# A planner that keeps GpSimd off VectorE's wide operations, and float64 conversion spread over fourteen chunks

## The chip, the cores and the metric

One core of one Trainium2 chip runs the whole program in one launch. The metric is the device time of that launch in microseconds (us), as the median of three runs. A difference of about 0.2% is the least that a measurement of this kernel can tell from no change.

## The reference

Three parts follow each other on 2304 tokens of width 512.

```
scores = q @ k.T / 8 - slope[h] * distance      # 8 heads, 576 positions, window 128, causal
attn   = softmax(scores) @ v                    # becomes x, 2304 x 512
P      = 8 rounds of row and column scaling of exp(x @ w_gate)
out    = sum over 8 experts of P[:, e] * (relu(x @ w1[e]) @ w2[e])       # 512 -> 1024 -> 512
result = leaky(out @ w_in, 0.01) @ w_out        # 512 -> 2048 -> 512
```

`w_in` and `w_out` come as float64 and are made into float32 on the chip, in 32 pieces of 128 x 512.

## The kernel before

**Work.** The two dense layers are 20 chunks of 512 hidden columns: 16 for the experts (two for each), 4 for the last layer. A chunk runs over five token groups (`PAIRS`: four of 512 tokens, one of 256), first through its half of the first matrix (`a_steps`, matmuls at L1089), then of the second (`b_steps`, L1205). Each product of 2 x 2 blocks is formed with 7 block products instead of 8 (`PRODUCTS`), and each of those is three fp16 matmuls, of high and low parts of both factors. A steady chunk is some 800 matmuls. TensorE (PE) runs nearly without a break; the other engines evict and combine its results and prepare the next chunk's weights.

**Who does what around TensorE.** ScalarE (ACT) copies the first block products out of PSUM (L1101 `q<-s`), VectorE (DVE) adds later ones (L1105 `sq<-s,q`) and writes the low parts of h (L1117). ACT and GpSimd (POOL) make high and low parts: L1158 and L1161 for h, L803 and L804 for weights. In `b_steps`, DVE adds results to the accumulators (L1218), or ACT and POOL share that (L1215, then L1216). POOL also makes the sums of weight blocks (L964).

**Float64 pieces** (`to_single`). A piece is loaded, and then runs through DVE L1018 (exponent bits), ACT L1021, DVE L1024 (sign), DVE L1029 (mantissa bits), ACT L1030, ACT L1036, POOL L1038 and L1042, and a store to DRAM. L1018, L1024 and L1029 read and write SBUF alone. `side_jobs(ci + 1, n)` puts n pieces beside the weights of the chunk after `ci`; before the change n is 3 for chunks 1 to 10 and 2 for chunk 11, and then the 32 pieces are done. The first piece of a chunk uses buffer `raw0` (in the rows `raw_173`), the others `raw1` (`raw_174`).

**The order.** The kernel is written as a stream of steps, and at its end a planner (`Plan`) sets the order of the instructions of each engine. `depend` finds who needs whom. `deadlines` gives each node the latest time by which it should end, counted back from matmuls that run without a break. `order` is a list scheduler: at each step it takes the engine that can go on first, and for it the ready node with the earliest deadline; `fix` writes the order into the program. Each engine then works through its own list in that order, and a late instruction holds up all that stands behind it on its engine.

`weigh` marks DVE nodes that work from SBUF to SBUF as `shared`: a price that `takes` raises when such a node would start while POOL is at work, and POOL's price rises when it would start while such a DVE node is at work. Both are prices in the planner's sums alone; nothing in the program makes POOL wait for DVE or DVE for POOL, other than data:

```python
            elif node["shared"] and gpsimd[0] <= t < gpsimd[1]:
                cost = max(cost, gpsimd[1] - t + cost - node["shared"])
            elif node["eng"] == "Pool" and port[0] <= t < port[1]:
                cost += max(0.0, port[1] - t - 140)
```

Of the kernel before, what the change touches and what calls it, by code (L numbers as in the profile page):

```python
# [30 lines left out]
class Plan:  # L31
# [13 lines left out]
    LANDING = 2000.0  # L45
    PER_NS = 350.0
    NEAR = 60.0

    def __init__(self, nc, tc, slots, before, after):
        self.tc = tc  # L50
# [192 lines left out]
    def deadlines(self, products):  # L243


        nodes = self.nodes
        n = len(nodes)
        ends, t, mode = {}, 0.0, "full"
        for i in products:
            t += nodes[i]["cost"] + self.TURN.get((mode, nodes[i]["mode"]), 0)  # L250
            mode = nodes[i]["mode"]
            ends[i] = t
        latest = [ends.get(i, t + 5000) for i in range(n)]
        left = [len(self.behind[i]) + len(self.softly[i]) for i in range(n)]
        room = dict.fromkeys(self.START, t + 5000)
        heap = [(-latest[i], -i) for i in range(n) if not left[i]]
        heapq.heapify(heap)
        while heap:
            i = -heapq.heappop(heap)[1]
            a = nodes[i]  # L260
            eng = a["eng"]
            if eng not in ("PE", "SP"):
                latest[i] = min(latest[i], room[eng])
                room[eng] = latest[i] - a["cost"] + self.START[eng]
            for k in a["before"] | a["starts"] | a["soft"]:
                b = nodes[k]
                end = latest[i] - a["cost"] + (b["cost"] if k in a["starts"] else -self.latency(b, a))
                latest[k] = min(latest[k], end)
                left[k] -= (k in a["before"]) or (k in a["starts"])
                left[k] -= k in a["soft"]  # L270
                if not left[k]:
                    heapq.heappush(heap, (-latest[k], -k))
        return latest

    def order(self, latest):
        nodes, behind = self.nodes, self.behind
        n = len(nodes)
        left = [len(node["before"]) + len(node["starts"]) for node in nodes]
        ready, free = [0.0] * n, dict.fromkeys(self.START, 0.0)
# [5 lines left out]
        empty = {tag: [0.0] * bufs for tag, bufs in self.room.items()}  # L285
        using = {name: len(u) for name, u in self.users.items()}
        closed = dict.fromkeys(self.users, 0.0)
        gpsimd, port, mode = (0.0, 0.0), (0.0, 0.0), "full"
        self.starts = [0.0] * n

        def since(i):

# [9 lines left out]
        def takes(i, t):  # L302

            node = nodes[i]
            cost = node["cost"]
            if node["eng"] == "PE":
                cost += self.TURN.get((mode, node["mode"]), 0)
            elif node["shared"] and gpsimd[0] <= t < gpsimd[1]:
                cost = max(cost, gpsimd[1] - t + cost - node["shared"])
            elif node["eng"] == "Pool" and port[0] <= t < port[1]:  # L310
                cost += max(0.0, port[1] - t - 140)
            return cost

        for _ in range(n):
            choices = []
            for e, w in waiting.items():
                when = [(x, i) for x, i in ((since(i), i) for i in w) if x is not None]
                if when:
                    choices.append((max(free[e], min(when)[0]), e, when))
            t, eng, when = min(choices)  # L320
            at = dict((i, x) for x, i in when)
            near = t + (self.NEAR if eng != "PE" else 0)
            pick = min((i for i in at if at[i] <= near), key=lambda i: (latest[i], i))
# [2 lines left out]
            if eng != "PE" and eng != "SP":  # L326

                for i in sorted((i for i in at if i != pick and at[i] < start + cost), key=lambda i: latest[i]):
                    s = max(at[i], t)
                    c = takes(i, s)  # L330
                    if (latest[i] < latest[pick] and max(at[i], start + cost) + nodes[i]["cost"] > latest[i]
                            and s + c + nodes[pick]["cost"] <= latest[pick]):
                        pick, start, cost = i, s, c
                        break
                if nodes[pick]["shared"] and cost > nodes[pick]["cost"] + 100:
                    other = [i for i in at if i != pick and not nodes[i]["shared"] and at[i] <= start + 100
                             and max(t, at[i]) + nodes[i]["cost"] + cost <= max(latest[pick], start + cost + 200)]
                    if other:
                        pick = min(other, key=lambda i: latest[i])
                        start = max(t, at[pick])  # L340
# [2 lines left out]
            end = start + cost  # L343
            if eng == "PE":
                mode = node["mode"]
            elif node["shared"]:
                port = (max(start, gpsimd[1]) if gpsimd[0] <= start < gpsimd[1] else start), end
            elif eng == "Pool":
                gpsimd = start, end
            self.starts[pick] = start  # L350
            free[eng] = end - (self.START[eng] if cost > 100 else 0)
            waiting[eng].remove(pick)
# [13 lines left out]
        self.length = end  # L366
        return orders

    def fix(self):
        follows = mybir.DependencyInfo(mybir.DependencyClass.NoSync, mybir.DependencyReason.DATA)  # L370
        products = [i for i, node in enumerate(self.nodes) if node["eng"] == "PE"]
        for picks in self.order(self.deadlines(products)).values():
            line = [ins for i in picks for ins in self.nodes[i]["ins"]]
            for a, b in zip(line, line[1:]):
                self.tc.add_manual_dep(b, a.name, follows, reason="order")


@with_exitstack
def attn_moe_kernel(
# [1022 lines left out]
    for n, u in enumerate(units + [None]):  # L1402
# [20 lines left out]
        if u is not None and ci >= 1:  # L1423
            if n and units[n - 1][0] != ci and ci != NCE:
                weigh(ci)
            if p == 4:
                side += side_jobs(ci + 1, 3 if ci < NCE - 1 else 0) if ci + 1 < NC else []
        if prev[0] == NCE:
            weigh_pair(*prev)
        seq = merge(a, b) if a else b  # L1430
# [63 lines left out]
```

## Time and profile before

| | |
|---|---|
| median of three runs | 1856.25 us (1854.02 to 1857.41) |
| the profiled execution | 1853.38 us, of which its span 1851.6 us |
| busy share of the span | PE 98%, DVE 74%, ACT 73%, POOL 71% |
| mean granted TensorE clock | 0.996 of full speed |

The profiled execution is 2.9 us shorter than the median and 0.6 us shorter than the fastest of the three runs. In the rows below, PE is the matmul engine, "idle before" in square brackets is the time for which the engine did nothing before that row, with what ended it, and PEclk is the share of TensorE's full clock that was granted (1.00 is 2.4 GHz, 0.50 is 1.2 GHz). The first 250 us hold attention, mixed with chunk 0; chunks 1 to 15 follow at some 84 us each; the last layer begins at about 1430 us.

### The profile page before, as it was taken

Reading aid. Unit: us, or ns where it says so; the run is one execution under the profiler, and the core shown is the slowest. Engines: PE = TensorE matmul, PEld = TensorE weight load, DVE = VectorE, ACT = ScalarE, POOL = GpSimd, SP = SyncE. Lnnn points to the kernel's source line nnn. Section 1 sums busy time; section 2 is a strip of 40 time slices with the busy share of each in tenths; the row PEclk is TensorE's granted clock in tenths of the full one; section 3 lists DMA queues with packets and bytes.
Section 4 is the critical chain, followed back from the end, with each engine's and each line's share of the span. In section 5 each row is a group of like instructions: output and inputs, shape, how many; then the busy total and the mean of one; then the engine's idle time right before and its main releaser. Section 6 shows DMA issues by size and latency. Waiting matters only on the chain.

```text
span 1851.6 us, 45040 instructions
## 1 busy us (share of the span) xinstructions
PE 1812.1 (98%) x17542; PEld 1603.7 (87%) x17542; DVE 1367.5 (74%) x3656; ACT 1348.8 (73%) x3099; POOL 1323.0 (71%) x1154
## 2 busy tenths in 40 slices
PE   8899999999999999999999999999999999999999
PEld 6677888889888888889888888889898888989888
DVE  7878677777777687777777776666676888687877
ACT  8988778767767766767767667666666789877664
POOL 3943878787869788787868777676667696776753
PEclk9999999999999999999999999999999999999999
DMA  8332020311112121202111110100000000101002
GB/s 296 109 115 76 4 81 28 87 37 62 53 47 67 32 74 37 86 27 72 53 47 53 47 52 30 47 24 24 24 24 34 15 24 24 47 1 47 1 33 72
DMA packets 61096, 97.81 MB, mean 53 GB/s; under 512 B 4561, under 2 KB 27601, under 8 KB 60881
## 3 DMA queue, kind: packets, MB, share of 16 engines
q1 hardware_dynamic: 60880, 94.93, 15.6%
q8 instruction: 137, 2.24, 0.5%
q14 instruction: 79, 0.64, 0.1%
HBM read 81.81 MB, written 13.11 MB: 51 GB/s over the span
## 4 chain that ended last, share of the span: by engine, by line
PE 76%; POOL 7%; ACT 6%; DVE 5%; DMA 4%; issue 2%; SPq 0%; POOLq 0%; DVEq 0%; ACTq 0%
PE t L1205 36%; PE s L1089 20%; PE sq L1089 15%; POOL w L804 3%; DMA raw<-in_moe_w_dram 3%; POOL h L1161 1%; PE s L570 1%; PE o L669 1%; PE pt L651 1%; ACT junk L937 1%; POOL xp L804 1%; DVE s L1117 1%; DVE raw L1018 1%; ACT raw L940 1%; DVE acc L1218 1%
## 5 line engine op out<-in xcount | busy, mean ns | idle before, releaser
L1205 PE MATMUL t<-w,h 128*128 128x256 f16 x7560 | 953.3, 273 | 7.5 <-ACT acc L1212 2.7
L1089 PEld LDWEIGHTS <-w 128*128 128x128 f16 x8400 | 757.0, 98 | 101.5 <-issue 22.9
L1205 PEld LDWEIGHTS <-h 128*128 128x128 f16 x7560 | 736.1, 98 | 97.1 <-issue 8.8
L1089 PE MATMUL s<-xp,w 128*128 128x256 f16 (+1 forms) x4872 | 591.3, 262 | 13.4 <-ACT q L1101 10.2
L1218 DVE SCALAR_TENSOR_TENSOR acc<-t,pu,acc 128x256 f32<-128x256 f32 x866 | 407.3, 479 | 173.5 <-PE t L1205 149.9
L1161 POOL TENSOR_TENSOR h<-s,h 128x1024 f16<-128x1024 f32 x180 | 386.2, 2145 | 135.1 <-ACT h L1158 95.4
L1089 PE MATMUL sq<-xp,w 128*128 128x256 f16 (+1 forms) x3528 | 429.9, 262 | 1.8 <-ACT q L1101 1.0
L1216 POOL TENSOR_TENSOR acc<-acc,part 128x256 f32<-128x256 f32 x322 | 238.9, 743 | 201.0 <-ACT part L1215 131.5
L804 POOL TENSOR_TENSOR w<-raw,w 128x512 f16<-128x512 f32 x240 | 274.7, 1162 | 28.8 <-ACT w L803 28.3
L1101 ACT ACTIVATE q<-s 128x256 f32<-128x256 f32 x364 | 138.6, 381 | 134.9 <-PE s L1089 132.3
L1158 ACT ACTIVATE h<-s 128x1024 f16<-128x1024 f32 x180 | 190.1, 1056 | 45.8 <-DVE s L1117 44.4
L1117 DVE SCALAR_TENSOR_TENSOR h<-sq,h 128x512 f16<-128x512 f32 x352 | 193.1, 553 | 34.0 <-ACT h L1136 24.4
L1215 ACT ACTIVATE part<-t,pu 128x256 f32<-128x256 f32 x322 | 152.1, 472 | 79.8 <-PE t L1205 75.0
L1105 DVE SCALAR_TENSOR_TENSOR sq<-s,q 128x256 f32<-128x256 f32 x176 | 75.8, 431 | 143.5 <-PE s L1089 86.3
L1105 DVE SCALAR_TENSOR_TENSOR sq<-sq,q 128x256 f32<-128x256 f32 x352 | 150.3, 427 | 38.1 <-PE sq L1089 33.6
L803 ACT ACTIVATE w<-raw 128x512 f16<-128x512 f32 x240 | 147.5, 631 | 12.1 <-PE s L1089 4.3
L1117 DVE SCALAR_TENSOR_TENSOR s<-sq,s 128x256 f32<-128x256 f32 x352 | 146.4, 416 | 0.7
L1136 ACT ACTIVATE h<-sq 128x512 f16<-128x512 f32 x176 | 104.9, 596 | 55.6 <-DVE sq L1105 46.5
L1117 DVE SCALAR_TENSOR_TENSOR s<-sq,q 128x256 f32<-128x256 f32 x352 | 137.1, 417 | 9.4 <-ACT q L1113 7.8
L940 ACT ACTIVATE raw<-raw,sr 128x512 f32<-128x512 f32 x160 | 109.7, 720 | 7.4 <-DVE sr L795 7.4
L937 ACT ACTIVATE junk<-raw 128x512 bf16<-128x512 f32 x160 | 100.4, 627 | 14.6 <-DMA raw<-in_moe_w_dram 9.1
L964 POOL TENSOR_TENSOR raw<-raw 128x512 f32<-128x512 f32 x80 | 102.4, 1280 | 0.0
(151 smaller groups left out, 1682.9 us busy)
## 6 DMA issues: line engine op xcount, KB each, us to landing
raw<-in_moe_w_dram SPq DMA_DIRECT2D x32, 768.0 KB, 4.7
k_t<-in_k_dram SPq DMA_DIRECT2D x16, 512.0 KB, 4.6
raw<-in_moe_w_dram SPq DMA_DIRECT2D x32, 256.0 KB, 3.6
raw<-in_moe_w_in_dram SPq DMA_DIRECT2D x16, 512.0 KB, 3.5
raw<-in_moe_w_out_dram SPq DMA_DIRECT2D x16, 512.0 KB, 3.5
q_t<-in_q_dram SPq DMA_DIRECT2D x18, 256.0 KB, 2.9
acc<-in_v_dram SPq DMA_DIRECT2D x18, 256.0 KB, 6.1
v_t<-in_v_dram SPq DMA_DIRECT2D x18, 256.0 KB, 2.7
```

What stands on the lines that cost most here:

```text
L803: nc.scalar.activation(out=hi, in_=src, func=AF.Copy)
L804: return nc.gpsimd.tensor_tensor(out=lo, in0=src, in1=hi, op=ALU.subtract)
L1089: nc.tensor.matmul(d[b][:, f, :], t[:, wp, kk, ft * P:(ft + 1) * P], XP[p][:, o, kk, xp, :], start=(i == 0 and f == 0 and j in FIRST), sto ...
L1101: nc.scalar.activation(out=q[:, k], in_=ps, func=AF.Copy, scale=CS)
L1105: nc.vector.scalar_tensor_tensor(out=block(k), in0=ps, scalar=CS, in1=q[:, k], op0=ALU.mult, op1=ALU.add)
L1117: nc.vector.scalar_tensor_tensor(out=out, in0=in0, scalar=sc, in1=in1, op0=op0, op1=op)
L1158: nc.scalar.activation(out=h[:, 3:7, 0, :], in_=d["s"], func=AF.Copy)
L1161: nc.gpsimd.tensor_tensor(out=h[:, 3:7, 1, :], in0=d["s"], in1=h[:, 3:7, 0, :], op=ALU.subtract)
L1205: nc.tensor.matmul(ps, h[:, o, hp, f, tt * P:(tt + 1) * P], w[:, wp, ft, :], start=(i == 0 and j in FIRST), stop=(i == 5), skip_group_chec ...
L1215: nc.scalar.activation(out=part, in_=ps, func=AF.Copy, scale=s)
L1216: nc.gpsimd.tensor_tensor(out=dst, in0=dst, in1=part, op=ALU.add)
L1218: nc.vector.scalar_tensor_tensor(out=dst, in0=ps, scalar=s, in1=dst, op0=ALU.mult, op1=ALU.add)
```

## The change

Three things in the planner and one number.

1. POOL's extra price is gone. In its place `order` remembers the last shared DVE node that no POOL node has followed yet (`holder`). The next POOL node starts, in the plan, 78 ns after that node's end. If its start lies less than 1500 ns after that node got the port, the pair goes into `turns`, and `fix` makes each pair a wait in the program (`DependencyClass.Sync`): POOL's instruction waits on a semaphore of DVE's.
2. When POOL is about to be given a node, `claim` looks whether a shared DVE node of more than 230 ns could start within 400 ns; if no urgent node of DVE or POOL would be late for it, DVE's node goes first. A shared DVE node that would start while POOL works, and has time, is put off until POOL is done.
3. `lag` is by how much TensorE is behind the plan without breaks; deadlines are compared with it added.
4. Pieces: 3 in each of chunks 1 to 4, 2 in each of chunks 5 to 14, again 32.

```diff
+    REACH = 400.0
+    GUARD = 1500.0
...
-            elif node["eng"] == "Pool" and port[0] <= t < port[1]:
-                cost += max(0.0, port[1] - t - 140)
...
+                if e == "DVE" and gpsimd[1] > free[e]:
+                    when = [(max(x, gpsimd[1]) if nodes[i]["shared"] and gpsimd[0] <= max(x, free[e]) < gpsimd[1]
+                             and latest[i] + lag > gpsimd[1] + nodes[i]["cost"] else x, i) for x, i in when]
...
+            if eng == "Pool":
+                if holder is not None:
+                    t = max(t, port[1] + self.TO["Pool"])
+                first = min((i for _, i in when if since(i) <= t + self.NEAR), key=lambda i: (latest[i], i), default=None)
+                wanted = self.claim(choices, latest, lag, free["DVE"], t, first)
+                if wanted is not None:
+                    eng, when = "DVE", [wanted]
+                    t = max(free["DVE"], wanted[0])
...
+                lag = max(lag, end - self.ends[pick])
             elif node["shared"]:
                 port = (max(start, gpsimd[1]) if gpsimd[0] <= start < gpsimd[1] else start), end
+                holder = pick
             elif eng == "Pool":
                 gpsimd = start, end
+                if holder is not None and start < port[0] + self.GUARD:
+                    self.turns.append((pick, holder))
+                holder = None
...
+    def claim(self, choices, latest, lag, free, t, first):
+        for _, e, when in choices:
+            if e == "DVE":
+                for x, i in sorted(when, key=lambda w: latest[w[1]]):
+                    a = self.nodes[i]
+                    start = max(free, x)
+                    if a["shared"] and a["cost"] > 230 and start <= t + self.REACH:
...
+                        return x, i
+        return None
...
+        after = mybir.DependencyInfo(mybir.DependencyClass.Sync, mybir.DependencyReason.DATA)
+        for i, k in self.turns:
+            self.tc.add_manual_dep(self.nodes[i]["ins"][0], self.nodes[k]["ins"][-1].name, after, reason="port")
...
-                side += side_jobs(ci + 1, 3 if ci < NCE - 1 else 0) if ci + 1 < NC else []
+                side += side_jobs(ci + 1, (3 if ci < 5 else 2) if ci < NCE - 1 else 0) if ci + 1 < NC else []
```

The changed file has 39 lines more above `to_single`: L1018 is L1057 there, L1024 L1063, L1029 L1068, L1161 L1200, L1216 L1255, L1218 L1257, L964 L1003, L804 L843.

**First place: the first piece of chunk 9.** POOL in the kernel before, around the weight sums that run there (`t` is a buffer for sums, `acc` an accumulator tile):

```order
L964 TENSOR_TENSOR t_12486<-raw_174 128x512 [waits Pool_49]
L1161 TENSOR_TENSOR h<-s,h 128x4x256 [waits Activation_49]
L964 TENSOR_TENSOR raw_174<-raw_174,t_12486 128x2x256 [waits Pool_49]
L1216 TENSOR_TENSOR acc_110<-acc_110,part 128x256 [waits DVE_49,Activation_49]
L964 TENSOR_TENSOR raw_174<-raw_174 128x2x256
L1216 TENSOR_TENSOR acc_112<-acc_112,part 128x256 [waits Activation_49]
L1038 TENSOR_TENSOR raw_173<-raw_173 128x512 [waits DMAHW7_49,Activation_49]
```

DVE in the kernel before, around that piece's three operations:

```order
L1218 SCALAR_TENSOR_TENSOR acc_109<-t_13893,pu,acc_109 128x256 [waits PE_49,Pool_49]
L1218 SCALAR_TENSOR_TENSOR acc_110<-t_13996,pu,acc_110 128x256 [waits PE_49]
L1018 TENSOR_SCALAR raw_173<-raw_173 128x512 [waits DMAHW1_49,Pool_49]
L1105 SCALAR_TENSOR_TENSOR sq<-sq,q 128x256 [waits PE_49,Activation_49]
L1218 SCALAR_TENSOR_TENSOR acc_109<-t_13893,pu,acc_109 128x256 [waits PE_49]
L1024 SCALAR_TENSOR_TENSOR raw_173<-raw_173,sign 128x512 [waits Activation_49]
L1029 TENSOR_SCALAR raw_173<-raw_173 128x512 [waits DMAHW2_49]
L1105 SCALAR_TENSOR_TENSOR sq<-s_13988,q 128x256 [waits DVE_49,PE_49,Activation_49]
```

POOL in the changed kernel, around the same piece (`w` is a weight tile):

```order
L1255 TENSOR_TENSOR acc_109<-acc_109,part 128x256 [waits Activation_49]
L1200 TENSOR_TENSOR h<-s,h 128x4x256 [waits DVE_49]
L843 TENSOR_TENSOR w_13868<-raw_173,w_13868 128x512 [waits Activation_49]
L1255 TENSOR_TENSOR acc_107<-acc_107,part 128x256 [waits DVE_49]
L1200 TENSOR_TENSOR h<-s,h 128x4x256 [waits DVE_49,Activation_49]
L1003 TENSOR_TENSOR raw_174<-raw_174,t_13725 128x2x256 [waits Pool_49]
L1255 TENSOR_TENSOR acc_110<-acc_110,part 128x256 [waits Activation_49]
L1003 TENSOR_TENSOR raw_174<-raw_174 128x2x256
L1077 TENSOR_TENSOR raw_173<-raw_173 128x512 [waits DMAHW1_49,Pool_49]
```

DVE in the changed kernel, there:

```order
L1156 SCALAR_TENSOR_TENSOR s<-sq,s 128x256 [waits DVE_49]
L1257 SCALAR_TENSOR_TENSOR acc_109<-t_13853,pu,acc_109 128x256 [waits PE_49,Pool_49]
L1057 TENSOR_SCALAR raw_173<-raw_173 128x512 [waits DMAHW3_49,DMAHW1_49,Pool_49]
L1156 SCALAR_TENSOR_TENSOR s<-sq,s 128x256 [waits DVE_49]
L1257 SCALAR_TENSOR_TENSOR acc_107<-t_13909,pu,acc_107 128x256
L1257 SCALAR_TENSOR_TENSOR acc_110<-t_13956,pu,acc_110 128x256 [waits PE_49]
L1063 SCALAR_TENSOR_TENSOR raw_173<-raw_173,sign 128x512 [waits Activation_49]
L1068 TENSOR_SCALAR raw_173<-raw_173 128x512 [waits DMAHW4_49]
L1144 SCALAR_TENSOR_TENSOR sq<-sq,q 128x256 [waits PE_49]
L1257 SCALAR_TENSOR_TENSOR acc_109<-t_13853,pu,acc_109 128x256
```

Before, POOL's `t`, `h`, `raw` stand behind each other with waits for ACT and POOL alone while L1018 is due on DVE. Now POOL's `acc_107` and the `h` behind it wait for DVE, and the sums that followed stand behind those two. In chunks 5 to 14 this pattern stands ten times.

**Second place: the first low parts of h, in attention.** POOL in the kernel before:

```order
L804 TENSOR_TENSOR w_735<-raw_174,w_735 128x512 [waits Activation_49]
L618 TENSOR_TENSOR pieces<-pieces 128x8 [waits DVE_49,PE_49]
L618 TENSOR_TENSOR pieces<-pieces 128x8 [waits Pool_49]
L1161 TENSOR_TENSOR h<-s,h 128x4x256 [waits Activation_49]
L804 TENSOR_TENSOR w_738<-raw_174,w_738 128x512 [waits Activation_49]
L804 TENSOR_TENSOR w_741<-raw_174,w_741 128x512 [waits Activation_49]
L1161 TENSOR_TENSOR h<-s,h 128x4x256 [waits Activation_49]
L538 MEMSET dist 64x192 [waits Activation_49,Pool_49]
```

POOL in the changed kernel:

```order
L657 TENSOR_TENSOR pieces<-pieces 128x8 [waits DVE_49,PE_49]
L657 TENSOR_TENSOR pieces<-pieces 128x8 [waits DVE_49,Pool_49]
L843 TENSOR_TENSOR w_729<-t_681,w_729 128x512 [waits DVE_49,Activation_49]
L1200 TENSOR_TENSOR h<-s,h 128x4x256 [waits DVE_49,Activation_49] x2
L843 TENSOR_TENSOR w_732<-raw_174,w_732 128x512 [waits Activation_49]
L843 TENSOR_TENSOR w_735<-raw_174,w_735 128x512 [waits Activation_49]
L843 TENSOR_TENSOR w_738<-raw_174,w_738 128x512 [waits Activation_49]
L843 TENSOR_TENSOR w_741<-raw_174,w_741 128x512 [waits Activation_49]
```

The two `h` now stand next to each other, ahead of the last four weight parts instead of among them, and `pieces`, `w` and `h` wait for DVE.

In the whole program 217 rows of POOL name a wait for DVE before, and 255 now; where POOL waited for DVE anyway, a row shows nothing new.

## Rows read from the trace of the kernel before

**Rows 1.** The page's busy times over the whole span.

```profile
PE 1812.1 (98%) x17542; PEld 1603.7 (87%) x17542; DVE 1367.5 (74%) x3656; ACT 1348.8 (73%) x3099; POOL 1323.0 (71%) x1154
```

**Rows 2.** Windows of 100 us: PE, PEld, DVE, ACT, POOL busy, PEclk, DMA share, GB/s.

```profile
600.00:700.00 100.00, 99.65 (x954) 89.47 (x953) 74.46 (x189) 72.01 (x156) 76.83 (x65) 1.00 0.20 64
...
900.00:1000.00 100.00, 94.75 (x888) 83.87 (x887) 75.32 (x174) 65.16 (x142) 75.25 (x64) 0.98 0.15 51
1000.00:1100.00 100.00, 97.42 (x955) 87.88 (x954) 74.04 (x180) 71.18 (x156) 78.11 (x66) 1.00 0.19 64
1100.00:1200.00 100.00, 99.78 (x975) 89.61 (x973) 67.31 (x179) 68.05 (x150) 66.55 (x58) 1.00 0.11 36
1200.00:1300.00 100.00, 99.79 (x957) 89.72 (x956) 68.90 (x184) 67.23 (x147) 70.67 (x60) 1.00 0.07 22
```

**Rows 3.** PE's waits: 900 to 1000 us, 1000 to 1100 us, the whole span.

```profile
PE s L1089 <- ACT q L1101: 4.4, 2, 2.2
...
PE s L1089 <- ACT q L1101: 2.6, 1, 2.6
...
PE t L1205 <- POOL h L1161: 1.6, 1, 1.6
```

**Rows 4.** Timeline from 902 us: start, us, engine, line, operation; POOL, DVE, ACT, PE.

```profile
902.13 1.29 POOL L964 TENSOR_TENSOR t<-raw 128x512 f32<-128x512 f32 x1
903.36 2.14 POOL L1161 TENSOR_TENSOR h<-s,h 128x1024 f16<-128x1024 f32 x1
905.45 1.28 POOL L964 TENSOR_TENSOR raw<-raw,t 128x512 f32<-128x512 f32 x1
...
903.05 3.96 DVE L1018 TENSOR_SCALAR raw<-raw 128x512 int32<-128x512 int32 x1
...
907.04 0.72 ACT L1021 ACTIVATE raw<-raw,shift 128x512 int32<-128x512 int32 x1 [4.03 <-DVE raw L1018]
907.67 0.36 ACT L1101 ACTIVATE q<-s 128x256 f32<-128x256 f32 x1
...
908.09 0.38 PE L1089 MATMUL s<-xp,w 128*128 128x256 f16 x2 [2.21 <-ACT q L1101]
```

**Rows 5.** Timelines of DVE and PE, one and two chunks later.

```profile
989.63 3.97 DVE L1018 TENSOR_SCALAR raw<-raw 128x512 int32<-128x512 int32 x1
...
994.68 0.49 PE L1089 MATMUL s<-xp,w 128*128 128x256 f16 x3 [2.21 <-ACT q L1101]
...
1076.50 4.33 DVE L1018 TENSOR_SCALAR raw<-raw 128x512 int32<-128x512 int32 x1
...
1081.91 0.49 PE L1089 MATMUL s<-xp,w 128*128 128x256 f16 x3 [2.58 <-ACT q L1101]
```

**Rows 6.** Short windows, columns as in rows 2.

```profile
80.00:90.00 10.00, 7.00 (x79) 4.90 (x73) 9.06 (x14) 7.96 (x23) 7.94 (x7) 0.71 0.42 133
...
184.00:190.00 6.00, 4.18 (x23) 2.91 (x23) 3.27 (x8) 4.94 (x11) 6.00 (x5) 0.72 0.00 0
990.00:1000.00 10.00, 7.79 (x57) 6.20 (x55) 7.77 (x11) 4.47 (x10) 6.26 (x6) 0.83 0.01 2
```

**Rows 7.** Timelines of POOL and DVE, one chunk before rows 4.

```profile
819.05 1.26 POOL L964 TENSOR_TENSOR t<-raw 128x512 f32<-128x512 f32 x1
820.28 2.31 POOL L1161 TENSOR_TENSOR h<-s,h 128x1024 f16<-128x1024 f32 x1
...
819.95 0.65 DVE L1018 TENSOR_SCALAR raw<-raw 128x512 int32<-128x512 int32 x1
```

**Rows 8.** All of L1018 (ns min/median/max), and one case of DVE's timeline.

```profile
L1018 DVE TENSOR_SCALAR raw<-raw x32: 414/650/4328, 234.1 to 1100.7; 128x512 int32<-128x512 int32 x32
...
672.55 2.29 DVE L1018 TENSOR_SCALAR raw<-raw 128x512 int32<-128x512 int32 x1
```

**Rows 9.** Timelines of DVE and PE in attention.

```profile
82.96 4.53 DVE L1117 SCALAR_TENSOR_TENSOR h<-q,h 128x768 f16<-128x768 f32 x2
...
83.09 0.66 PE L651 MATMUL pt<-ident,e 128*128 128x128 f32 x4 [1.15 <-DVE pb L656]
...
86.73 2.96 PE L1205 MATMUL t<-w,h 128*128 128x256 f16 x13 [1.56 <-POOL h L1161]
```

More of the change, by code (lines that the diff above doesn't have):

```diff
@@ L252, in deadlines @@
             ends[i] = t
+        self.ends = ends
         latest = [ends.get(i, t + 5000) for i in range(n)]
@@ L287, in order @@
         closed = dict.fromkeys(self.users, 0.0)
-        gpsimd, port, mode = (0.0, 0.0), (0.0, 0.0), "full"
+        gpsimd, port, mode, holder = (0.0, 0.0), (0.0, 0.0), "full", None
         self.starts = [0.0] * n
+        self.turns = []
+        lag = 0.0
         def since(i):
@@ L330, in order @@
                     c = takes(i, s)
-                    if (latest[i] < latest[pick] and max(at[i], start + cost) + nodes[i]["cost"] > latest[i]
-                            and s + c + nodes[pick]["cost"] <= latest[pick]):
+                    if (latest[i] < latest[pick] and max(at[i], start + cost) + nodes[i]["cost"] > latest[i] + lag
+                            and s + c + nodes[pick]["cost"] <= latest[pick] + lag):
                         pick, start, cost = i, s, c
@@ L336, in order @@
                     other = [i for i in at if i != pick and not nodes[i]["shared"] and at[i] <= start + 100
-                             and max(t, at[i]) + nodes[i]["cost"] + cost <= max(latest[pick], start + cost + 200)]
+                             and max(t, at[i]) + nodes[i]["cost"] + cost <= max(latest[pick] + lag, start + cost + 200)]
                     if other:
@@ L367, in order @@
         return orders
+    def claim(self, choices, latest, lag, free, t, first):
[5 more added lines that the diff above has]
+                    if a["shared"] and a["cost"] > 230 and start <= t + self.REACH:
+                        late = start + a["cost"]
+                        if any(k != i and max(y, late) + self.nodes[k]["cost"] > latest[k] + lag and latest[k] < latest[i]
+                               and y <= late for y, k in when):
+                            return None
+                        if first is not None and latest[first] < latest[i] and late + self.nodes[first]["cost"] > latest[first] + lag:
+                            return None
+                        return x, i
+        return None
     def fix(self):
```

## The prediction

> **What bounds the kernel now.** I read the page's busy times first. PE is busy for 1812.1 of 1851.6 us, and no other engine passes 74% [rows 1]. So at most 39.5 us of idle PE, and whatever TensorE lost at half clock, can be won back; shorter work on another engine is worth nothing by itself. The windows of 100 us show where those microseconds lie. Around 650 and 1250 us PE is busy for 99.65 and 99.79 of 100 us, with and without float64 pieces beside it; from 900 to 1100 us it falls to 94.75 and 97.42 [rows 2]. That is the one place in the steady part with something to win.
>
> PE's waits say what is missing there: `s` at L1089 waits for ACT's `q` at L1101, twice for 4.4 us together and once for 2.6 us [rows 3], 7.0 us in all. The timeline gives the chain, to be read backwards. PE starts at 908.09 after 2.21 us of nothing. ACT's L1101, which released it, is a copy of 0.36 us that stood in ACT's list behind L1021, and L1021 had made ACT idle for 4.03 us because it waited for DVE's L1018 [rows 4]. L1018 is shown with 3.96 us; over all 32 pieces its shortest is 0.414 us and its median 0.650 [rows 8]. It begins at 903.05, while POOL is in `t`, and ends only after POOL has also finished `h` and `raw`, three operations without a gap, until 906.73 [rows 4]. One and two chunks later the same happens with 3.97 and 4.33 us, and PE loses 2.21 and 2.58 us [rows 5]. In the middle one the clock follows: from 990 to 1000 us it was granted at 0.83 [rows 6], part of the time at 1.2 GHz instead of 2.4, after PE had stood still.
>
> The rows of chunk 8 tell that it is a race. There too L1018 arrives some 0.36 us before `t` ends (819.95 against 820.31; in rows 4, 903.05 against 903.42), with the same `h` behind. It takes 0.65 us, and this time `h` is the one that is stretched, to 2.31 instead of 2.14 us [rows 7, 4]. Nothing in the order decides who goes first at the end of `t`.
>
> **The change, part by part.**
>
> *The waits.* In chunk 9 POOL's `acc_107` and the `h` behind it now wait for DVE, as the order shows, and the sums that L1018 sat through come later. So POOL can no longer run three operations past a waiting L1018; at worst it finishes the one it is in. A wait of that size is harmless: at 672.55 an L1018 of 2.29 us, behind one `h`, left no gap in PE [rows 8]. I take all three places as gone: 7.0 us of idle PE [rows 3], and the clock's share, 10 us at 0.83, which is 1.7 us of full clock [rows 6]. Together 8.7 us. Bounds: nothing, if the race comes back in another form, and 8.7.
>
> *What the waits cost.* POOL's rows that name a wait for DVE go from 217 to 255. If each of the 38 added rows stood for a median L1018, 0.65 us [rows 8], POOL would lose 25 us of the 528.6 us in which it has nothing to do [rows 1]. What is queued behind a waiting POOL instruction is `h`, for which PE's `t` waits. In the whole span PE waited for POOL's `h` once, 1.6 us [rows 3], at 86.73 in attention [rows 9], and never in chunks 1 to 19. So I cost the waits at nothing; the cover is how far `h` is ahead of PE, which no row gives, and if it is used up the price is that of rival A.
>
> *The pieces.* Chunks 5 to 10 lose one piece each, chunks 12 to 14 gain two each; chunk 11 keeps two. Three pieces in a chunk cost PE at most 99.79 - 99.65 = 0.14 us per 100 us [rows 2], so six pieces moved from one place to another come to some 0.2 us less and 0.2 us more: nothing. A chunk of two pieces is in the trace already: behind its lost race at 1076.50 [rows 5] the window from 1100 us, with the last piece in it, has PE busy for 99.78 [rows 2]. The loads and stores of a piece move with it and number the same. The first piece of a chunk still uses `raw0` and still meets POOL's sums of the other weights, so this part alone would not take the race away.
>
> *Attention.* The planner remakes the order of the first 250 us too. Two stretches there lose PE time and clock. From 80 to 90 us PE is busy for 7.00 us at a granted 0.71: 3.0 us idle and 2.9 us of clock. From 184 to 190 us it is 4.18 of 6 us at 0.72: 1.8 and 1.7 us [rows 6]. That is 9.4 us. Of the gaps in the first, 1.15 us ended with DVE's L656 and 1.56 us with POOL's `h`, while two L1117 on DVE took 4.53 us beside POOL's `h` and `w` [rows 9]; in the new order the two `h` stand together ahead of four weight parts. So part of the 5.9 us there should go. But every list is different there, and a new place of the same kind can appear. No row of before shows the new order, so I bound it by what is there: a gain of 9.4 us, a loss of 5.9 us, one more place like the first. I take a gain of 2.0 us, about a third of the first stretch, since one of its two gaps hangs on what was moved.
>
> *Sum.* 1853.4 us, the profiled execution, less 8.7 and 2.0 is 1842.7 us. That execution lies 2.9 us below the median of the three runs. The four executions together have their middle at 1855.1 us (between 1854.02 and 1856.25), and I put the result against that: 1855.1 - 10.7 = **1844.4 us**.
>
> **A rule that speaks against the change.** In rows 4, L1018 is issued inside `t` and still lets `h` and `raw` go first; the row decides, and the sum above rests on it. The Trainium skill, "SBUF — State Buffer", section "SBUF: two separate sides", says that VectorE and GpSimd share one pair of SBUF ports as an exclusive lock, and that whichever starts first holds it for its whole instruction while the other is blocked. By that alone an operation issued before `h` would go before `h`, about 0.4 us late, and waits that keep POOL behind it would win nothing of the 8.7 us. Rows 7 agree with the rule, rows 4 and 5 do not.
>
> **Rivals.**
>
> *A, slower.* The waits hold POOL where it was not held, and the fourteen chunks are now so alike that one bad place repeats. The place: `acc_107` and then `h` wait for DVE's piece, L1057 waits for its load and for POOL, and whatever makes DVE late now makes `h` late, then PE's `t`. It decides once `h` loses its lead on PE. The price in a chunk is between the 1.6 us of the one known case [rows 3] and the 2.2 to 2.6 us of a lost race [rows 5]. At 2.2 us in ten chunks that is 22 us, less the 8.7: 1855.1 + 13.3 = 1868 us. For it: `h` stands right behind the waits. Against it: POOL has a good quarter of its time free [rows 1], and POOL made PE wait only once. Chance 0.10.
>
> *B, no change: the race moves.* A wait only stops POOL's operation that the plan puts behind L1057. If DVE comes to L1057 one POOL operation sooner than planned, it sits through `w`, `acc` and whatever is ahead of the wait, as it sat through `h` and `raw`. Then three or so chunks in ten lose 2.2 to 2.6 us [rows 5] as now, or attention gives back what the chunks win: some 1853 to 1857 us. For it: arrivals differ by less than 0.1 us between a won and a lost race [rows 7, 4]. Against it: the last operation ahead of the wait is a single `w`, not a train with an `h` in it. Chance 0.08.
>
> *C, no change: the waits do nothing*, because POOL and DVE take turns in the order of issue, or because data already made POOL wait there. The three long L1018 would then come from something else that both versions have: 1853 to 1855 us. This is what the Trainium skill's rule above would make of it. Only rows 7 speak for it [rows 7]. Chance 0.04.
>
> **How the numbers follow.** The forecast, that most of the three stalls goes and attention moves by a few microseconds, has the remaining chance, 0.78; with the bounds above it spans 1855.1 - 8.7 - 9.4 = 1837 us up to about 1852 us (8.7 gained, 5.9 given back). The range from 1837 to 1855 us takes in that and half of B and C, and leaves out A, the upper half of B and C, and a little below: under 0.2. What a measurement can tell from no change is about 0.2%, 3.7 us, so below 1852.5 us counts as faster: 0.78; B and C are the same: 0.12; A is slower: 0.10.
>
> **What would show it.** Right: no L1057 longer than about 2.6 us (one POOL `h` and itself), PEclk 1.00 and PE above 99.5 of 100 us in every window from 300 to 1400 us, no wait of PE for ACT's `q` above 1 us in chunks 5 to 14, and some POOL rows whose idle time now ends with DVE's `raw`. Wrong: PE's `t` waiting for POOL's `h` in the chunks (A), L1057 of 3 to 4 us again (B), or long L1057 with the waits in place and no POOL operation between (C). The attention term is wrong if the windows 0 to 100 and 100 to 200 us have less PE time than before.

## The result, and the profile after

| | before | after |
|---|---|---|
| median of four runs | 1856.83 us (1854.02 to 1868.97) | 1835.76 us (1835.07 to 1840.13) |
| ratio, with its 95% interval | | 0.9879 (0.9833 to 0.9925) |
| the profiled execution, its span | 1853.38, 1851.6 us | 1836.15, 1834.4 us |
| mean granted clock of that execution | 0.996 | 0.998 |

Faster, as forecast, but by more: 21.1 us between the medians and 17.2 us between the profiled executions, against 10.7. The time lies 1.2 us under the range's lower end.

I read it in the order of the prediction. First the page's busy times after, to hold against [rows 1].

```profile
PE 1807.2 (99%) x17542; PEld 1603.1 (87%) x17542; DVE 1326.3 (72%) x3656; ACT 1353.9 (74%) x3099; POOL 1309.0 (71%) x1154
```

PE is idle for 1834.4 - 1807.2 = 27.2 us, where it was 39.5: 12.3 us less. The mean clock went from 0.996 to 0.998 of the span, 7.4 to 3.7 us of full clock, another 3.7 (each clock is rounded to 0.001 and so good to 0.9 us). That makes 16.0 of the 17.2 us; the rest, with the clock's part, lies in PE's busy time, which fell by 4.9 us with the same 17542 matmuls. DVE is busy for 41 us less with the same 3656 instructions: an operation that waits for POOL while it is "running" is counted as busy.

Where the idle time went, by windows of 100 us after (columns as in [rows 2]).

```profile
0.00:100.00 100.00, 89.41 (x859) 67.77 (x861) 75.05 (x297) 89.71 (x280) 60.03 (x82) 0.98 0.62 206
100.00:200.00 100.00, 95.04 (x1033) 75.96 (x1030) 70.94 (x257) 85.87 (x257) 50.16 (x57) 0.98 0.23 70
...
600.00:700.00 100.00, 99.45 (x955) 89.50 (x953) 70.49 (x189) 71.23 (x156) 72.31 (x62) 1.00 0.12 38
...
900.00:1000.00 100.00, 99.73 (x980) 89.85 (x978) 69.82 (x180) 71.25 (x156) 78.48 (x68) 1.00 0.16 57
1000.00:1100.00 100.00, 99.75 (x974) 89.95 (x971) 69.58 (x181) 69.40 (x152) 70.69 (x62) 1.00 0.15 51
```

The two windows from 900 us had 94.75 and 97.42 [rows 2]; they now have 99.73 and 99.75, 7.3 us more. A window of fixed times holds more work in the faster kernel, so the stages are compared by equal work: these windows are cut where PE has started the same matmuls in both kernels (the number behind x). The three are, within some matmuls, attention with chunk 0, chunks 1 to 15, and the last layer. Before:

```profile
0.00:254.91 254.91, 234.41 (x2400) 188.30 (x2401) 192.55 (x666) 214.33 (x627) 154.52 (x178) 0.98 0.37 118
254.91:1441.95 1187.04, 1174.37 (x11303) 1053.73 (x11301) 852.69 (x2140) 833.94 (x1810) 892.96 (x752) 1.00 0.15 47
1441.95:1851.60 409.65, 403.32 (x3844) 361.66 (x3841) 322.26 (x850) 300.53 (x664) 275.56 (x226) 1.00 0.08 28
```

And after:

```profile
0.00:249.64 249.64, 233.98 (x2400) 188.45 (x2401) 183.57 (x667) 213.85 (x622) 148.60 (x176) 0.99 0.37 119
249.64:1422.55 1172.91, 1169.55 (x11302) 1053.08 (x11301) 821.72 (x2139) 840.05 (x1815) 884.84 (x754) 1.00 0.15 48
1422.55:1834.40 411.85, 403.62 (x3844) 361.57 (x3841) 321.04 (x850) 300.01 (x664) 275.61 (x226) 1.00 0.08 28
```

Attention is 5.3 us shorter, the chunks 14.1, and the last layer is 2.2 us longer: together 17.2. In the chunks 9.3 us are idle time. The other 4.8 us are in PE's busy time, of which the half clock of [rows 6] explains 1.7. So 5.1 us of the chunks' gain lie outside the three lost races and their clock, and 3.1 of these the idle time does not show. Rows of PE at a first piece before, with DVE's second and third operation beside them, show how a wait hides in the busy time:

```profile
572.85 0.82 PE L1089 MATMUL sq<-xp,w 128*128 128x256 f16 x6
573.51 0.82 PE L1205 MATMUL t<-w,h 128*128 128x256 f16 x6
574.53 0.81 PE L1089 MATMUL s<-xp,w 128*128 128x256 f16 x6 [0.20 <-DVE sq L1105]
...
570.98 1.75 DVE L1024 SCALAR_TENSOR_TENSOR raw<-raw,sign 128x512 int32<-128x512 int32 x1
572.65 1.49 DVE L1029 TENSOR_SCALAR raw<-raw 128x512 int32<-128x512 int32 x1
```

Rows of six matmuls start 0.66 us apart here but are shown with 0.82. Behind the held L1024 and L1029 the next one starts after 1.02 us: 0.36 us are lost, and 0.20 are shown as idle. So the idle time, which I use below for windows from 300 to 1400 us, is a low count of what PE loses. Those windows, before and after:

```profile
300.00:1400.00 1100.00, 1088.12 (x10454) 976.39 (x10452) 790.55 (x1980) 768.43 (x1669) 835.97 (x703) 1.00 0.14 47
...
300.00:1400.00 1100.00, 1097.20 (x10580) 987.94 (x10578) 772.26 (x2004) 782.38 (x1689) 834.96 (x711) 1.00 0.15 48
```

The timelines of POOL, DVE and ACT at a first piece, after, show the mechanism; they answer to [rows 4].

```profile
892.91 1.17 POOL L843 TENSOR_TENSOR w<-raw,w 128x512 f16<-128x512 f32 x1
894.65 0.73 POOL L1255 TENSOR_TENSOR acc<-acc,part 128x256 f32<-128x256 f32 x1 [0.57 <-DVE raw L1057]
896.82 2.13 POOL L1200 TENSOR_TENSOR h<-s,h 128x1024 f16<-128x1024 f32 x1 [1.45 <-DVE raw L1068]
...
894.15 0.42 DVE L1057 TENSOR_SCALAR raw<-raw 128x512 int32<-128x512 int32 x1
...
895.60 0.74 DVE L1063 SCALAR_TENSOR_TENSOR raw<-raw,sign 128x512 int32<-128x512 int32 x1
896.26 0.42 DVE L1068 TENSOR_SCALAR raw<-raw 128x512 int32<-128x512 int32 x1
...
894.60 0.72 ACT L1060 ACTIVATE raw<-raw,shift 128x512 int32<-128x512 int32 x1
```

L1057 starts right behind POOL's `w` and takes 0.42 us, its bare length. POOL stands still for 0.57 us until it is done, then does one short `acc`, and stands still again for 1.45 us until L1063 and L1068 are done; `h` starts 0.14 us after L1068. ACT's L1060 goes on at once, where its counterpart had made ACT idle for 4.03 us. The first and the last of the three operations over all pieces (ns min/median/max):

```profile
L1057 DVE TENSOR_SCALAR raw<-raw x32: 412/418/1373, 231.2 to 1332.1; 128x512 int32<-128x512 int32 x32
...
L1068 DVE TENSOR_SCALAR raw<-raw x32: 414/419/423, 234.8 to 1333.9; 128x512 int32<-128x512 int32 x32
```

L1018 had 414/650/4328 [rows 8]. POOL pays for it; its waits over the span (us in total, times, longest):

```profile
POOL acc L1255 <- DVE raw L1068: 24.8, 16, 3.6
...
POOL h L1200 <- DVE raw L1068: 15.7, 11, 1.4
```

That is 40 us of standing still behind L1068 alone, and PE does not notice. POOL's idle time as a whole did not grow: 1834.4 - 1309.0 = 525.4 us, where it was 528.6. The largest of PE's waits after, the load of `k_t` at the start left out:

```profile
PE t L1244 <- ACT acc L1251: 3.9, 3, 2.9
PE t L1244 <- DVE acc L1257: 2.8, 7, 0.9
PE pt L690 <- ACT pb L693: 2.8, 3, 1.1
PE xt L916 <- DVE k L828: 1.6, 1, 1.6
PE s L1128 <- ACT q L1140: 1.2, 1, 1.2
```

No wait of `t` for POOL's `h` is in the list; the one of 1.6 us [rows 3] is gone.

### The profile page after: what moved, and what is told of

It is laid out like the page before. It is cut to its first block, busy times and chain, and to the rows that moved or that the text cites. A ratio compares the mean times of both kernels' runs of the same rounds, so it can differ in the third digit from the quotient of the medians.

```text
span 1834.4 us, 45055 instructions
## 1 busy us (share of the span) xinstructions
PE 1807.2 (99%) x17542; PEld 1603.1 (87%) x17542; DVE 1326.3 (72%) x3656; ACT 1353.9 (74%) x3099; POOL 1309.0 (71%) x1154
## 4 chain that ended last, share of the span: by engine, by line
PE 68%; ACT 2%; DVE 2%; DMA 2%; POOL 2%; issue 1%; DVEq 0%; ACTq 0%; POOLq 0%
PE t L1244 34%; PE s L1128 19%; PE sq L1128 15%; POOL w L843 1%; DMA raw<-in_moe_w_dram 1%; DMA raw<-win 1%; DVE s L1156 1%; ACT junk L976 0%; DVE sx L930 0%; DMA raw<-in_moe_w_out_dram 0%; DVE acc L1257 0%; ACT acc L917 0%; POOL acc L1255 0%; ACT h L1197 0%; PE xt L916 0%
## 5 line engine op out<-in xcount | busy, mean ns | idle before, releaser
L1257 DVE SCALAR_TENSOR_TENSOR acc<-t,pu,acc 128x256 f32<-128x256 f32 x866 | 405.0, 479 | 193.8 <-PE t L1244 151.8
L1200 POOL TENSOR_TENSOR h<-s,h 128x1024 f16<-128x1024 f32 x180 | 383.8, 2132 | 101.9 <-ACT h L1197 46.3
L1255 POOL TENSOR_TENSOR acc<-acc,part 128x256 f32<-128x256 f32 x322 | 234.2, 729 | 217.2 <-ACT part L1254 98.4
L843 POOL TENSOR_TENSOR w<-raw,w 128x512 f16<-128x512 f32 x240 | 274.0, 1162 | 66.1 <-ACT w L842 65.8
L1003 POOL TENSOR_TENSOR raw<-raw 128x512 f32<-128x512 f32 x80 | 102.0, 1274 | 0.4 <-DVE dg L819 0.4
```

Of the source, the lines that this page charges most:

```text
L843: return nc.gpsimd.tensor_tensor(out=lo, in0=src, in1=hi, op=ALU.subtract)
L1200: nc.gpsimd.tensor_tensor(out=h[:, 3:7, 1, :], in0=d["s"], in1=h[:, 3:7, 0, :], op=ALU.subtract)
L1255: nc.gpsimd.tensor_tensor(out=dst, in0=dst, in1=part, op=ALU.add)
L1257: nc.vector.scalar_tensor_tensor(out=dst, in0=ps, scalar=s, in1=dst, op0=ALU.mult, op1=ALU.add)
```

## The experiments

The first four runs take the change apart; the later ones follow what these left open. To compare the chunks I use PE's idle time from 300 to 1400 us, read from one window of each profile (11.9 us before, 2.8 after): there nearly the same work runs, at full clock but for the 1.7 us that follow the second lost race. Where it says "by equal work", the stage is cut by matmuls as above.

**The waits alone, on the old order.**

```diff
+                if holder is not None and start < port[0] + self.GUARD:
+                    self.turns.append((pick, holder))
...
+        for i, k in self.turns:
+            self.tc.add_manual_dep(self.nodes[i]["ins"][0], self.nodes[k]["ins"][-1].name, after, reason="port")
```

> The planner and pieces of before, with the added waits alone: the planner keeps its old prices and order, and only records, by the same rule as the change, which POOL instruction follows a shared DVE node within 1500 ns; those pairs become waits. Theory W (the waits give the gain): no L1018 over 2.7 us in any chunk, the 8.7 us of chunks 9 to 11 come back and the small PE gaps of the other chunks shrink, 1841 to 1847 us. Theory O (the new order gives it): the order is the old one, so 1852 to 1858 us. Theory P (fewer pieces in a chunk): the same, 1852 to 1858 us.

Measured: 1846.44 us, ratio 0.9961 (0.9945 to 0.9976). The window of the chunks:

```profile
300.00:1400.00 1100.00, 1096.87 (x10560) 984.47 (x10558) 784.25 (x2000) 776.99 (x1685) 838.74 (x712) 1.00 0.14 47
```

and one of PE's longest gaps, in the timeline of attention:

```profile
88.23 2.60 PE L1214 MATMUL t<-w,h 128*128 128x256 f16 x13 [2.97 <-POOL h L1170]
```

3.1 us idle in the chunks: with the old order and the old pieces, the waits take away nearly all that the whole change takes away there, by equal work 12.4 of the 14.1 us. Attention does not gain (256.5 us by equal work, where before had 254.9): rival A's mechanism stands there once, `t` waiting 2.97 us for POOL's `h`, where before it was 1.56 [rows 9].

**The new order without its waits.**

```diff
-        for i, k in self.turns:
-            self.tc.add_manual_dep(self.nodes[i]["ins"][0], self.nodes[k]["ins"][-1].name, after, reason="port")
```

> The changed kernel without the added waits: its order and pieces stay, and nothing but data holds POOL. W: L1057 of 3 to 4 us comes back in some of chunks 5 to 14, 2 to 3 us of PE each, and 1842 to 1852 us. O: nothing changes, 1834 to 1838 us, and no L1057 over 2.7 us. P: 1834 to 1840 us.

Measured: 1857.25 us, ratio 1.0028 (1.0006 to 1.0050), a little slower than before. The window of the chunks:

```profile
300.00:1400.00 1100.00, 1088.22 (x10463) 974.63 (x10461) 785.16 (x1982) 773.78 (x1672) 828.40 (x700) 1.00 0.14 47
```

and the timelines of POOL, DVE and PE at one place (L1060 and L1065 are the sign and the mantissa operation):

```profile
403.16 2.37 POOL L1197 TENSOR_TENSOR h<-s,h 128x1024 f16<-128x1024 f32 x1 [2.07 <-ACT h L1194]
...
402.81 0.73 DVE L1060 SCALAR_TENSOR_TENSOR raw<-raw,sign 128x512 int32<-128x512 int32 x1
403.47 2.34 DVE L1065 TENSOR_SCALAR raw<-raw 128x512 int32<-128x512 int32 x1
...
406.89 0.81 PE L1125 MATMUL sq<-xp,w 128*128 128x256 f16 x6 [2.50 <-ACT q L1137]
```

11.8 us idle in the chunks, as much as before, spread over other places; the time lies above the range of theory W, and the first operation of a piece, which was to take 3 to 4 us again, takes at most 1.47 us from 300 us on. The plan had put `h` behind L1065; without the wait POOL starts `h` as soon as its data are there, 0.31 us ahead of L1065, and L1065 takes 2.34 us instead of 0.42. The order alone is worth nothing: it is an order for an engine that waits. These rows agree with the rule of the Trainium skill ("SBUF — State Buffer", "SBUF: two separate sides"), by which the first to start holds the port for its whole instruction: `h` ends at 405.53, L1065 0.28 us later.

**The pieces, alone and left out.** Before with the new number of pieces, and after with the old one:

```diff
-side_jobs(ci + 1, 3 if ci < NCE - 1 else 0)
+side_jobs(ci + 1, (3 if ci < 5 else 2) if ci < NCE - 1 else 0)
```

> The planner of before with 3 pieces in each of chunks 1 to 4 and 2 in each of chunks 5 to 14. W and O: the race stays, since each chunk's first piece still meets POOL's sums; 1850 to 1858 us. P: 1836 to 1843 us.

> The changed planner, waits and all, with 3 pieces in each of chunks 1 to 10 and 2 in chunk 11. W and O: 1834 to 1841 us, with no L1057 over 2.7 us. P: 1846 to 1856 us.

Measured: alone 1849.65 us, ratio 0.9980 (0.9959 to 1.0000); left out 1836.75 us, ratio 0.9912 (0.9878 to 0.9946), beside 1835.76 for the full change. With the waits the pieces do nothing that can be told apart. Alone they may give some 0.2%; the profile then has one lost race (L1018 with 4.29 us at 571.10, PE idle 2.53 us behind it) instead of three, and PE is idle for 7.9 us in the chunks. One execution can't say whether that is the pieces or chance.

**Waits in the chunks alone, and in attention alone.** The change, with its pairs kept only behind, or only up to, 215 us of the plan:

```diff
-                if holder is not None and start < port[0] + self.GUARD:
+                if holder is not None and start < port[0] + self.GUARD and start > 215000.0:
...
+                if holder is not None and start < port[0] + self.GUARD and start <= 215000.0:
```

> The changed kernel with the added waits left out where the planner sets POOL's instruction before 215 us of its own time, that is in attention; order and pieces as in the change. If attention's gain of 4.6 us comes from the new order, 1834 to 1838 us, as the changed kernel. If it comes from the waits, chunk 1 begins 3 to 6 us later and the time is 1838 to 1842 us.

> The changed kernel with the added waits in attention alone, the complement of the run with waits in the chunks alone. If the two sets of waits add up (no waits 1857.3, chunks alone 1844.6, both 1835.8), this one lies at 1857.3 - 8.8, 1846 to 1851 us, with chunk 1 beginning at about 247.6 us of the span. If they do not add, because each set needs the other to keep POOL and DVE where the plan has them, 1852 to 1858 us.

Measured: in the chunks alone 1844.57 us, above both expected ranges, ratio 0.9949 (0.9934 to 0.9964); in attention alone 1856.68 us, ratio 1.0005 (0.9990 to 1.0021). From no waits at all (1857.25) the chunks' waits give 12.7 us, and their stage by equal work falls from 1187.7 to 1173.9. Attention's waits give 0.6 us without them and 8.8 on top of them. That the two do not add is not shown: by the ratios the two shares are 0.2% and 0.7%, and the intervals allow them to be equal. The window of 10 us that had 7.00 us of PE at 0.71 [rows 6], with waits in the chunks alone:

```profile
80.00:90.00 10.00, 7.57 (x98) 5.87 (x96) 9.18 (x20) 7.38 (x20) 5.69 (x5) 0.90 0.09 28
```

and after:

```profile
80.00:90.00 10.00, 9.61 (x127) 7.66 (x125) 8.79 (x25) 9.42 (x26) 8.27 (x6) 1.00 0.21 59
```

In all six profiles that have the change's order of attention and its waits (two with the longer guard), PE has 9.60 or 9.61 us there; in the two that have the order without the waits, 7.54 and 7.57. So 2 us of attention's gain are the waits, shown. By equal work four profiles with the change's order, waits and guard in attention end it at 249.5 to 252.7 us, three with the old order at 254.9 to 256.2, and the two without the waits at 251.8 (granted clock 1.00) and 257.6 (0.97). The rest of the 8.8 us lies partly with the clock: the four runs with waits in the chunks alone have a mean clock of 0.9960, the change 0.9980, 3.7 us. But the clock doesn't follow from the program alone: the kernel without any waits has the same attention, and its ten runs have 0.9975. What sets it there stays open.

**Eleven waits only, on the old order**: POOL's next instruction waits behind L1032 (the first operation) of each chunk's first piece, and nowhere else.

```diff
+                if holder is not None and start < port[0] + self.GUARD and self.first_bits(nodes[holder]):
```

> The kernel before with eleven waits and nothing else: the POOL instruction behind L1018 of each chunk's first piece waits for it. If the three lost races are worth what their PE gaps and half clock say, no L1018 of a first piece is over 1.5 us, 8 to 9 us of chunks 9 to 11 come back and attention stays: 1843 to 1848 us, as with all waits alone. If the gain of the waits comes from many small places, 1849 to 1856 us.

Measured: 1849.65 us, ratio 0.9973 (0.9957 to 0.9989). PE is idle for 9.5 us in the chunks. POOL's, DVE's and PE's timelines in one of them (L1038 is the sign operation here, L1043 the mantissa's):

```profile
656.33 2.13 POOL L1175 TENSOR_TENSOR h<-s,h 128x1024 f16<-128x1024 f32 x1 [0.43 <-DVE raw L1032]
...
655.53 0.66 DVE L1032 TENSOR_SCALAR raw<-raw 128x512 int32<-128x512 int32 x1
...
656.98 2.03 DVE L1038 SCALAR_TENSOR_TENSOR raw<-raw,sign 128x512 int32<-128x512 int32 x1
658.94 1.48 DVE L1043 TENSOR_SCALAR raw<-raw 128x512 int32<-128x512 int32 x1
...
660.81 0.82 PE L1103 MATMUL s<-xp,w 128*128 128x256 f16 x6 [0.48 <-DVE sq L1119]
```

and the largest of PE's waits over the span:

```profile
PE s L1103 <- DVE sq L1119: 5.5, 10, 1.0
```

The three big stalls are gone, but the wait only moves what POOL makes DVE miss: `h` now starts behind L1032, so L1038 sits through it for 2.03 us and L1043 through part of the sum behind it. PE is idle for 0.48 us here, and for 5.5 us in ten such places. In the run with all waits on the old order the sign operation is held as long (2.03 us at 653.95), but the mantissa operation behind it takes 0.41 us, and PE has no gap; so it is the third operation, held on top, that costs. By equal work the eleven waits win 3.7 us in the chunks, and all waits 12.4: freeing the first operation alone keeps little of what the lost races cost. This is rival B's mechanism, in a kernel other than the one it was meant for.

**No claim.** The change without the rule that lets DVE go first in the plan:

```diff
-                wanted = self.claim(choices, latest, lag, free["DVE"], t, first)
+                wanted = None
```

> The changed kernel without claim: POOL's node is planned when its turn comes, even where a shared DVE node could start within 400 ns; putting off DVE nodes, the 78 ns behind a holder and the waits stay. If the waits and the putting off carry the gain, 1834 to 1840 us. If DVE must be let in first, its shared operations wait longer for POOL (more than five L1057 or L1068 over 0.8 us) and the time is 1840 to 1850 us.

Measured: 1852.75 us, ratio 1.0006 (0.9987 to 1.0024). The window of the chunks:

```profile
300.00:1400.00 1100.00, 1091.07 (x10475) 977.33 (x10473) 786.17 (x1988) 767.91 (x1672) 825.81 (x700) 1.00 0.14 47
```

and POOL's and DVE's timelines in one of the chunks:

```profile
574.32 2.14 POOL L1200 TENSOR_TENSOR h<-s,h 128x1024 f16<-128x1024 f32 x1
576.41 1.28 POOL L1003 TENSOR_TENSOR raw<-raw 128x512 f32<-128x512 f32 x1
...
574.98 2.99 DVE L1057 TENSOR_SCALAR raw<-raw 128x512 int32<-128x512 int32 x1
```

8.9 us idle, and a time above the expected 1840 to 1850 us. The waits are there, but they guard only what the plan puts behind L1057; `h` and `raw` stand ahead of it, L1057 comes while `h` runs, and `raw` goes past it too. That is rival B's mechanism, and it shows what `claim` is for: something must first put DVE's operation in front, and then the wait keeps it there. In the run of the waits alone the old price on POOL is still in force and may do that; no run takes it out there.

**No lag, and lag off at the end.** `lag` left out, and `lag` set to 0 from 1385 us of the plan on:

```diff
-                lag = max(lag, end - self.ends[pick])
+                lag = max(lag, end - self.ends[pick]) if start < 1385000.0 else 0.0
```

> The changed kernel with lag held at zero, so that deadlines are compared as if TensorE had run without breaks. If lag lets the planner tell urgent from not urgent in and after attention, the gain there shrinks: 1838 to 1846 us. If it does not matter, 1834 to 1838 us.

> The changed kernel with lag set back to zero once the planner's own time is past 1385 us, that is for the last layer alone. If lag is what costs the last layer some 2 us against the kernel before, that part ends 2 to 3 us sooner after chunk 15 (about 419.6 instead of 422.9 us) and the time is 1832 to 1835 us. If it is something else, 1835 to 1838 us.

Measured: without it 1837.80 us, ratio 0.9913 (0.9899 to 0.9928); off at the end 1835.18 us, ratio 0.9889 (0.9859 to 0.9918). Neither can be told from the change. In the profiles the last layer gains, though: the window from 1450 to 1650 us after is

```profile
1450.00:1650.00 200.00, 195.39 (x1860) 174.74 (x1859) 158.15 (x426) 163.61 (x367) 154.56 (x124) 1.00 0.06 23
```

and with lag off at the end

```profile
1450.00:1650.00 200.00, 198.12 (x1888) 177.32 (x1887) 163.02 (x438) 166.44 (x373) 156.64 (x126) 1.00 0.06 23
```

where before it had 196.95. By equal work the last layer takes 410.8 to 411.8 us in the three profiles of the change, of its planner with the old pieces and of the longer guard, 408.5 to 408.8 in the three with `lag` out or off there, and 409.7 before. So the change's loss of 2.2 us in the last layer comes with `lag`.

**A longer guard, and both.** `GUARD` of 4000 instead of 1500 ns; and lag off at the end with the longer guard in attention alone:

```diff
-    GUARD = 1500.0
+    GUARD = 4000.0
```

> The changed kernel with GUARD at 4000 ns instead of 1500, so that POOL also waits for a shared DVE node that is planned well before it. If what is left of DVE's operations held by POOL (two L1063 of 2.0 us, some L819 over 1 us) still costs PE, 1832 to 1835 us; if not, 1835 to 1838 us; if the added waits hold POOL where it need not be held, above 1838 us.

> The changed kernel with lag set back to zero for the last layer (as in the run of that alone) and GUARD at 4000 ns in attention alone (before 215 us of the planner's time), 1500 elsewhere. If the parts add up as the two runs show them, attention ends at 246.0 us without half clock, chunks 1 to 14 stay as in the changed kernel, and the last layer takes 419.9 instead of 422.9 us: 1831 to 1834 us, faster than the changed kernel. If the clock in attention is a matter of chance and not of the waits, 1833 to 1837 us, with a granted clock of 0.996 to 0.999.

Measured: 1836.28 us, ratio 0.9894 (0.9868 to 0.9920), and 1834.47 us, ratio 0.9888 (0.9866 to 0.9910). The longer guard has the highest clock of all, 0.9995 over its four runs, which is 2.8 us better than the change, and the same time: by equal work its attention ends 1.6 us sooner, with 2.2 us more of idle time, and its chunks take 2.3 us longer. Both together have the lowest median, 1.3 us under the change, and intervals that overlap; no version is shown to be better than the change.

## Why the prediction was right, and where it was not

| step | predicted | profiled execution, by equal work |
|---|---|---|
| three lost races, with their clock | -8.7 | -9.0 (7.3 idle, 1.7 clock) |
| what the waits cost | 0 | 0 in PE, 40 us of POOL's standing still |
| other places in the chunks | 0 | -5.1 (2.0 idle, 3.1 in busy time) |
| attention | -2.0 | -5.3 |
| last layer | 0 | +2.2 |
| sum | -10.7 | -17.2 |

Against the forecast of 1844.4 us, 6.5 us of the 8.6 are in these terms; 1.7 come from counting from 1855.1 us, when the profiled execution that the rows are of took 1853.4, and 0.4 from the profiled execution after, which is above its median.

**The race** was right in its mechanism, its places and its size. The waits alone take it away on the old order, and without them the new order leaves as much idle time in the chunks as before. So rival C, that the waits do nothing, is refuted. The prediction had read more into the rule of the Trainium skill than that section says: the rule names the holder, and is silent on who follows when the holder ends. There POOL's next operation went past a waiting DVE in [rows 4] and in the run without `claim`.

**The waits' cost** was right at nothing for PE, and the bound in POOL's time too low: 25 us was taken, and L1068 alone made POOL stand for 40, all of it inside the idle time that POOL had anyway. The cover held, since POOL's `h` was never late for `t`. Rival A did come, once, but in attention and only with the old order.

**The step that failed most is the other chunks**, "That is the one place in the steady part with something to win". They were taken at nothing because PE is busy for 99.65 and 99.79 of 100 us there, and they gave 5.1 us, 3.1 of them in what the profile counts as busy. The cause is the one that the prediction had found: before, in first pieces without a lost race, L1024 is held to 1.75 us and L1029 to 1.49, as at 570.98; after, no L1068 takes more than 0.42 us. The median of the first operation fell from 0.650 to 0.418 us. That it is the waits is shown by the new order with and without those of the chunks: 1173.9 and 1187.7 us for the same stage.

**The second is attention**, "I take a gain of 2.0 us, about a third of the first stretch"; it gave 5.3. The first stretch gave nearly all it had: from 7.00 us of PE at 0.71 [rows 6] to 9.61 at 1.00, 2.6 us of idle time and 2.9 of clock; but 1.8 us of clock were lost anew just ahead of it, from 50 to 80 us, granted at 0.94 where before had 1.00. I had asked which gap hangs on a moved instruction, and named but did not price DVE's two L1117 of 4.53 us beside POOL's `h` and `w` [rows 9], held as L1018 was, which is what the waits act on. With waits in the chunks alone two operations of the same line, of 128x256, still take 3.32 us there, at 82.97. The second stretch did not gain: PE's longest wait is there now (ACT's `acc` before `t`, 2.94 us at 181.62), and the window from 100 to 200 us has 95.04 us of PE instead of 95.45. Of the 5.3 us, 2 are shown to be the waits; how the rest divides between order and granted clock is open.

**The last layer** was not priced at all, and lost 2.2 us to `lag`, which hides a part of the two misses.

**The signs in the profile** held but for one: L1057 stays under 1.4 us, PE waits for `q` at most 0.5 us at a time in the chunks, POOL names DVE's `raw`, and every window from 300 to 1400 us is above 99.5 but that from 600 us, with 99.45. The sign for attention was a poor one: its second window has less PE time, and attention as a whole gained.

**The range** ended at 1837.0 us because its lower bound took all that attention's two named stretches had lost, but from the chunks only the 8.7 us of the lost races, where they gave 14.1. Against the medians of before in the later measurements, 1852.65 to 1856.06 us, the change gains 16.9 to 20.3 us; before itself spreads from 1848.12 to 1863.40 us in 25 runs, the change over 5 us in four.

## What to carry to other kernels

When two engines get in each other's way without any data between them, a planner's price is a wish: the program needs a wait that holds the order, and an order that puts the right one first. Here the new order without the waits won nothing, the waits on the old order some 0.4%, and both together 1.2%. Put the wait behind the last of the operations that must stay together, or the loss moves to the next one. A cause found in one stage should be searched for, by its rows, in all stages before the others are costed at nothing or a third. And compare stages by equal work: an engine's busy share hid a fifth of what the chunks won.

## What the runs showed of the hardware that was not expected

A DVE operation that waits for POOL can be passed by POOL's next operations: by two more in [rows 4], by one in the run without `claim` (L1057 issued at 574.98, POOL's `raw` started at 576.41 and went first). And the same attention program ran with quite different clocks: the first 250 us were granted 1.00 in the profile of the kernel without any waits, and 0.97 in that of the kernel with waits in the chunks alone, which is the same there. A higher clock gave less than its share: the kernel with the longer guard was granted 1.000 instead of 0.998 in its profiled execution, some 3.7 us, and ended attention 1.6 us sooner; PE waited for ACT's `acc` around 181 us for 2.93 us there and 2.94 in the change.
